# A three-stage fp32 block on one core: the identity matrix loaded earlier, head loads in two parts, no sums on GpSimd

## Chip, cores and metric

The kernel runs on one core of one Trainium2 chip. The metric is the device time of one execution in microseconds (us), the median of several.

## What is computed

Attention with a local window and a few global keys, then a token and channel mixer, then a gated block, on batch 2, 8 heads, 768 tokens, head size 64 (so 512 channels). Cut to what matters:

```python
scores = (q @ k.T) / 8 - slope[h] * dist            # kept where key < n_global or 0 <= i-j < n_local
a = softmax(scores);  x = heads_to_channels(a @ v)  # x: (2, 768, 512)
u = x + (relu(x.T @ w_tok1) @ w_tok2).T             # token mixing
y = u + relu(u @ w_ch1) @ w_ch2                     # channel mixing, 1536 wide
h = relu(y @ w_in); g, v = h[:, :512], h[:, 512:]
out = (g * (w_spatial @ layernorm(v) + b)) @ w_out
```

The weights arrive as 64-bit floats (w_spatial as 32-bit) and are split on the chip into a high and a low part, so every large product is three matmuls (`mm3`, lines 341 to 343).

## The kernel before

**Stages.** The first stage, about the first 107 us, is attention with the token mixing (`tok`) woven in. The 16 heads are 8 pairs; a pair has three units of 256 queries (`unit`), and `group` takes two units at a time, so there are 12 groups. Per unit TensorE makes scores (L479), VectorE adds the bias and finds the maximum (L496), ScalarE does exp (L500), TensorE transposes the result with the identity matrix `ident` (L506), ScalarE or VectorE copies it out as `pt` (L346). Per group, TensorE multiplies the copies with the values (L534, "main", and L544, "rest"), and the result goes back through another transpose (L567). Then come channel mixing for batch 0 and batch 1 (`ch`, to about 340 us) and the gated block (`mlp2`).

**What sets the order.** Every piece of work is an `Op` with its possible engines and their costs in us. `Plan.run` simulates the engines and writes the program in the order in which it places the pieces; each engine then executes its own row in that order, whatever arrives when. `RAW_AT` holds earliest planned starts for loads, `free` the time at which an engine is first free in the plan, `dma()` the planned time of a transfer (plus a lag of 2.1 us on SP). Eighty dummy matmuls of 256 columns (L593, "fillers") stand in the plan wherever TensorE has nothing else.

**Loads.** All are issued by SP, in order. The first head pair is loaded by hand in `build` (L240 to L247) in four pieces into `first`: two pieces of queries and keys, a third piece of keys, then the values (1088 KB); `ident` (64 KB) comes last. The other seven pairs are loaded by `load_raw` (L441), one transfer of 1936 KB each, into two buffers `raw`: a load can start when the pair two before it has been used up by L544. Weights pass through staging buffers (L386) and are split by ScalarE (L387, L388) and VectorE (L389 to L394, L352).

**Sums.** `tts` names the engines for a sum or difference of two tensors: GpSimd or VectorE. Residual sums at the end of `ch` and some splits use it (all at L352). At the end of `ch` for one batch, `ch` for the other batch goes on, and its `L786` on VectorE feeds TensorE.

Of the kernel before, what the change touches and what calls it, by code (L numbers as in the profile page):

```python
# [51 lines left out]

WARM = 9

RAW_AT = {(0, 1): 5.5, (0, 2): 12.5}
IDLE = 80, 4.0, 0.2

SWITCH, TURN = 0.16, 2.0
# [37 lines left out]
class Plan:  # L96
# [41 lines left out]
    def run(self):  # L138
        after = {}
        for q in self.slots.values():  # L140
            for b in q:
                if b.first is None:
                    continue
                for u in b.users:
                    if u is not b.first:
                        after.setdefault(u, set()).add(b.first)
                if b.opener is not None and b.opener.plan is self:
                    b.first.deps.add(b.opener)
                if b.evicts is not None:
                    b.first.deps.update(b.evicts.users)  # L150
                if b.prior is not None and b.prior.first is not b.first:
                    after.setdefault(b.first, set()).add(b.prior.first)
                b.first.deps.discard(b.first)
        for o in self.ops:
            both = {d for d in o.deps | after.get(o, set()) if d.plan is self}
            o.left = len(both)
            for d in both:
                d.kids.append((o, d in o.deps))
        order = [o for o in self.ops if o.left == 0]
        wait = {o: o.left for o in self.ops}  # L160
        for o in order:
            for k, _ in o.kids:
                wait[k] -= 1
                if wait[k] == 0:
                    order.append(k)
        for o in reversed(order):
            e, c = min(o.where, key=lambda x: x[1])
            o.rank = c + max((k.rank + (self.LAG[e] if data else 0.0) for k, data in o.kids), default=0.0)
            o.key = (PK * o.pri - o.rank, o.n)
        free = dict.fromkeys(self.LAG, 4.0)  # L170
        avail = [o for o in self.ops if o.left == 0]
        mode = "full"
        while avail:
            best, t_min, picks = None, None, []
            for o in avail:
                _, s, e, c = min((max(free[e], o.ready) + c * (1.0 + o.lam.get(e, 0.0)), max(free[e], o.ready), e, c) for e, c in o.where)
                picks.append((s, o, e, c))
            t_min = min(p[0] for p in picks)
            s, o, e, c = min((p for p in picks if p[0] <= t_min), key=lambda p: (p[1].key[0] + TURN * (p[1].mode not in (None, mode)), p[1].n))
            avail.remove(o)  # L180
            if o.mode not in (None, mode):
                c += SWITCH
            mode = o.mode or mode
            free[e] = s + c
            o.fn(e)
            for k, data in o.kids:
                if data:
                    same = len(k.where) == 1 and k.where[0][0] == e and e != "SP"
                    k.ready = max(k.ready, s + c + (0.0 if same and e == "PE" else 0.06 if same else self.LAG[e]))
                k.left -= 1  # L190
                if k.left == 0:
                    avail.append(k)
        assert all(o.left == 0 for o in self.ops)
# [10 lines left out]
def pool(n):  # L204
    return ("POOL", n * 0.0023 + 0.05)


def dma(nbytes):
    return ("SP", max(nbytes / 360e3, 0.5))


def mm(n, count):
# [3 lines left out]
def build(tc, A, out):  # L216
    nc = tc.nc
    V, SC, SY = nc.vector, nc.scalar, nc.sync
    with ExitStack() as top:
# [19 lines left out]
        with tc.manual_schedule():  # L239
            SY.dma_start(nt, A["n"].partition_broadcast(P))  # L240
            load0 = lambda c0, c1: SY.dma_start(raw0[:, c0:c1], A["qkv"][0, 0, :, c0:c1])
            SY.dma_start(rj, A["rj"])
            load0(512, 1056)
            load0(0, 512)
            load0(1056, QK)
            load0(QK, RAW)
            SY.dma_start(ident, A["ident"])  # L247
            V.memset(zero, 0.0)
            for x in shift:
                V.memset(x, 0.0)  # L250
            V.memset(epst, 1e-6)
            SC.activation(warm, epst, AF.Exp)
            with tc.tile_pool(name="dp", bufs=1, space=bass.MemoryType.PSUM) as dp:
                dummy = dp.tile([P, 512], F32, name="dummy")
                for _ in range(WARM):
                    nc.tensor.matmul(dummy, lhsT=zero, rhs=zero[:, 0:1].broadcast_to([P, 512]), start=True, stop=True)

            gl, ll = nt[:, 0:1], nt[:, 2:3]
            V.tensor_scalar(out=fl[:, 0:1], in0=gl, scalar1=0.0, scalar2=None, op0=ALU.is_ge)
            V.tensor_scalar(out=fl[:, 1:2], in0=ll, scalar1=1.0, scalar2=None, op0=ALU.is_ge)  # L260
            V.scalar_tensor_tensor(out=fl[:, 0:1], in0=gl, scalar=float(GMAX), in1=fl[:, 0:1], op0=ALU.is_le, op1=ALU.mult)
            V.scalar_tensor_tensor(out=fl[:, 1:2], in0=ll, scalar=float(LMAX), in1=fl[:, 1:2], op0=ALU.is_le, op1=ALU.mult)
            V.tensor_tensor(out=fi, in0=fl[:, 0:1], in1=fl[:, 1:2], op=ALU.mult)
            V.tensor_copy(fl[:, 2:3], gl)
            V.tensor_copy(fl[:, 3:4], ll)
            gl, ll = fl[:, 2:3], fl[:, 3:4]
            far = stgp.tile([P, 1024], BF16, tag="c", name="far")[:, :BW]
            glb = stgp.tile([P, 1024], BF16, tag="a", name="glb")[:, :BW]
            V.tensor_scalar(out=far, in0=rj[:, 0], scalar1=ll, scalar2=BIG, op0=ALU.is_ge, op1=ALU.mult)
            V.tensor_scalar(out=glb, in0=rj[:, 1], scalar1=gl, scalar2=BIG, op0=ALU.is_ge, op1=ALU.mult)  # L270
            V.tensor_tensor(out=far, in0=far, in1=rj[:, 0], op=ALU.max)
            V.scalar_tensor_tensor(out=dist, in0=glb, scalar=ll, in1=far, op0=ALU.max, op1=ALU.min)
# [10 lines left out]
class Arm:  # L283
# [68 lines left out]
        self.eng[e].tensor_tensor(out=o, in0=a, in1=b, op=op)  # L352

    def tts(self, n):
        return [pool(n), dve(n)]

    def split(self, hi, lo, src, n, rk, hk, lk):

# [72 lines left out]
    def load_raw(self, b, hp):  # L431
# [5 lines left out]
            self.rawk[b, hp] = None  # L437
            return
        r = self.raws[b, hp] = self.buf("att", "raw", [P, RAW], F32, 2)
        self.rawk[b, hp] = (r,)  # L440
        o = self.plan.op([dma(P * RAW * 4)], lambda e: self.SY.dma_start(r(), self.A["qkv"][b, hp, :, :RAW]), [], [(r,)], RAWP if (b, hp) != (0, 1) else None)  # L441
        o.ready = RAW_AT.get((b, hp), 0.0)

    def band_bias(self, b, h):
        bias = self.bias[b, h] = self.buf("att", f"bias{h % 2}", [P, BW], F32, 2)
# [17 lines left out]
    def scores(self, units):  # L463
# [4 lines left out]
        for k, (b, hp, u) in enumerate(units):  # L468
            tiles = self.tiles(u)

            def make(e, k=k, b=b, hp=hp, tiles=tiles):
                raw = self.raws[b, hp]
                for t, o, w in tiles:
                    for x in range(2):
                        k0 = S + (160 * t - P + D * x if t else 0)
                        q0 = q_at(t) + D * x
                        for i in range(2):
# [1 line left out]
                            T.matmul(banks[k][i]()[x * D:x * D + D, o:o + w], lhsT=r[:, q0:q0 + D], rhs=r[:, k0:k0 + w],  # L479
                                     start=True, stop=True)  # L480

            self.plan.op([("PE", sum(w for _, _, w in tiles) * 0.00175)], make, [self.rawk[b, hp] or ("raw0", "ab"[u > 0])],
                         [(x,) for x in banks[k]], mode="quarters")
        return banks

# [27 lines left out]
    def group(self, units):  # L513
# [31 lines left out]
                                     rhs=pts[k][h]()[r, 2 * P + x * D:2 * P + x * D + D], start=False,  # L545
                                     stop=(x == 1 and k == max(z for z in range(2) if units[z][2] or j)))

        rk = [self.rawk[b, hp] or ("raw0", "v") for b, hp, _ in units]
        ps = [(p,) for x in pts for p in x]
        op([("PE", 0.88)], main, ps + rk, [(c,) for c in cs], mode="columns")  # L550
        op([("PE", 0.44)], rest, ps + rk, [(c,) for c in cs], mode="quarters")
# [490 lines left out]
```

## Time and profile before

| | us |
|---|---|
| median of 3 runs | 484.67 (484.59 to 484.98) |
| the profiled execution | 484.22, of it span 482.3 |
| TensorE busy | 470.4 |
| VectorE busy | 292.3 |
| ScalarE busy | 208.5 |
| GpSimd busy | 29.7 |

The span runs from the first to the last instruction. Matmuls are pipelined, so TensorE counts as busy while it moves through waits shorter than a matmul's length; a wait that shows as idle is a true one. Fillers count as busy too. A wait in brackets behind a row is the idle time of that engine just before it, and who ended it.

### The profile page before, as it was taken

Reading aid. Unit: us, or ns where it says so; the run is one execution under the profiler, and the core shown is the slowest. Engines: PE = TensorE matmul, PEld = TensorE weight load, DVE = VectorE, ACT = ScalarE, POOL = GpSimd, SP = SyncE. Lnnn points to the kernel's source line nnn. Section 1 sums busy time; section 2 is a strip of 40 time slices with the busy share of each in tenths; the row PEclk is TensorE's granted clock in tenths of the full one; section 3 lists DMA queues with packets and bytes.
Section 4 is the critical chain, followed back from the end, with each engine's and each line's share of the span. In section 5 each row is a group of like instructions: output and inputs, shape, how many; then the busy total and the mean of one; then the engine's idle time right before and its main releaser. Section 6 shows DMA issues by size and latency. Waiting matters only on the chain.

```text
span 482.3 us, 8996 instructions
## 1 busy us (share of the span) xinstructions
PE 470.4 (98%) x3557; PEld 413.0 (86%) x3557; DVE 292.3 (61%) x773; ACT 208.5 (43%) x527; POOL 29.7 (6%) x29
## 2 busy tenths in 40 slices
PE   7999999999999999999999999999999999999996
PEld 4788888789988888888888888888999988899985
DVE  4899998779988986012986854236961512722520
ACT  3999898897645544110333501113521122411121
POOL 0110001000000000000500000003330000000000
PEclk9999999999999999999999999999999999999999
DMA  7944927413343442000033311110000011000012
GB/s 275 376 171 167 371 91 278 187 63 119 116 148 114 146 152 97 0 1 1 0 102 128 121 65 37 63 34 0 2 0 1 1 67 65 1 0 2 0 45 93
DMA packets 10993, 44.66 MB, mean 93 GB/s; under 512 B 1344, under 2 KB 1856, under 8 KB 9920
## 3 DMA queue, kind: packets, MB, share of 16 engines
q1 hardware_dynamic: 10944, 44.01, 25.5%
q8 instruction: 30, 0.49, 0.4%
q14 instruction: 19, 0.16, 0.1%
HBM read 40.86 MB, written 3.15 MB: 91 GB/s over the span
## 4 chain that ended last, share of the span: by engine, by line
PE 82%; DVE 7%; DMA 6%; ACT 1%; issue 1%; POOL 1%; SPq 0%; ACTq 0%; DVEq 0%; POOLq 0%
PE p L341 23%; PE p L343 23%; PE p L342 23%; PE p L506 3%; PE p L479 3%; PE p L534 2%; DMA raw<-in_qkv 2%; DMA raw<-in_w_in 2%; DVE first L352 2%; PE p L544 1%; DMA raw<-in_wt 1%; PE p L593 1%; PE p L567 1%; DVE uy0l L352 1%; PE p L738 1%
## 5 line engine op out<-in xcount | busy, mean ns | idle before, releaser
L341 PE MATMUL p<-raw,w 128*128 128x512 f32 (+1 forms) x192 | 64.8, 338 | 0.0
L342 PE MATMUL p<-raw,w 128*128 128x512 f32 (+1 forms) x192 | 64.7, 337 | 0.0
L785 ACT ACTIVATE raw<-p 128x512 fp32r<-128x512 f32 (+1 forms) x48 | 23.6, 491 | 95.0 <-PE p L343 88.1
L343 PE MATMUL p<-raw,w 128*128 128x512 f32 (+1 forms) x192 | 64.6, 337 | 0.0
L786 DVE SCALAR_TENSOR_TENSOR raw<-p,raw 128x512 fp32r<-128x512 f32 (+1 forms) x48 | 26.0, 552 | 37.4 <-ACT raw L785 37.1
L341 PE MATMUL p<-uy1h,w 128*128 128x512 f32 (+2 forms) x128 | 43.3, 338 | 1.6 <-DVE raw L786 1.6
L343 PE MATMUL p<-uy1h,w 128*128 128x512 f32 (+2 forms) x128 | 43.2, 337 | 0.0
L343 PE MATMUL p<-uy0h,w 128*128 128x512 f32 (+2 forms) x128 | 43.1, 337 | 0.0
L342 PE MATMUL p<-uy1l,w 128*128 128x512 f32 (+2 forms) x128 | 43.1, 337 | 0.0
L342 PE MATMUL p<-uy0l,w 128*128 128x512 f32 (+2 forms) x128 | 43.1, 337 | 0.0
L341 PE MATMUL p<-uy0h,w 128*128 128x512 f32 (+2 forms) x128 | 43.1, 336 | 0.0
L500 ACT ACTIVATE e<-e,nm 128x192 f32<-128x192 f32 (+1 forms) x96 | 41.9, 445 | 1.3 <-DVE nm L496 1.3
L387 ACT ACTIVATE c<-raw 128x512 bf16<-128x512 bf16 x42 | 28.3, 673 | 30.1 <-DMA raw<-in_w_in 17.4
L343 PEld LDWEIGHTS p<-raw,w 128*128 128x128 f32 x192 | 36.1, 188 | 4.2
L341 PEld LDWEIGHTS p<-raw,w 128*128 128x128 f32 x192 | 36.1, 188 | 4.1
L342 PEld LDWEIGHTS p<-raw,w 128*128 128x128 f32 x192 | 36.1, 188 | 4.0
L352 DVE TENSOR_TENSOR c<-p,bsp 128x384 f32<-128x384 f32 x16 | 8.9, 558 | 39.7 <-PE p L343 39.7
L496 DVE CUSTOM_DVE_ANT_0 e<-p,bias 128x192 f32<-128x192 f32 (+1 forms) x96 | 27.4, 341 | 5.1 <-PE p L479 5.1
L394 DVE SCALAR_TENSOR_TENSOR a<-raw,q 128x512 f32<-128x512 uint32 x42 | 29.0, 691 | 0.5
L352 DVE TENSOR_TENSOR a<-a,c 128x512 f32<-128x512 f32 x42 | 28.8, 686 | 0.4
L388 ACT ACTIVATE c<-raw 128x512 bf16<-128x512 bf16 x42 | 28.1, 670 | 0.0
L341 PEld LDWEIGHTS p<-uy1h,w 128*128 128x128 f32 x128 | 24.1, 188 | 4.5 <-DVE raw L786 2.4
(163 smaller groups left out, 1086.5 us busy)
## 6 DMA issues: line engine op xcount, KB each, us to landing
raw<-in_qkv SPq DMA_DIRECT2D x7, 1936.0 KB, 9.8
raw<-in_wch SPq DMA_DIRECT2D x24, 512.0 KB, 3.7
raw<-in_w_in SPq DMA_DIRECT2D x8, 512.0 KB, 4.1
raw<-in_wt SPq DMA_DIRECT2D x6, 512.0 KB, 5.4
out<-a SPq DMA_DIRECT2D x11, 256.0 KB, 2.0
raw<-in_w_sp SPq DMA_DIRECT2D x6, 384.0 KB, 2.9
raw<-in_w_out SPq DMA_DIRECT2D x4, 512.0 KB, 3.9
first<-in_qkv SPq DMA_DIRECT2D x1, 1088.0 KB, 7.2
```

The costliest lines, as they stand in the source:

```text
L341: T.matmul(o, lhsT=w[0], rhs=x[0], start=first, stop=False)
L342: T.matmul(o, lhsT=w[0], rhs=x[1], start=False, stop=False)
L343: T.matmul(o, lhsT=w[1], rhs=x[0], start=False, stop=last)
L352: self.eng[e].tensor_tensor(out=o, in0=a, in1=b, op=op)
L387: op([act(n)], lambda e: self.SC.mul(pw(), top(), 2.0 ** -112), [(w,)], [(c, 0)])
L388: op([act(n)], lambda e: self.SC.activation(sg(), top(), AF.Sign), [(w,)], [(c, 1)])
L394: op([dve(n)], lambda e: V.scalar_tensor_tensor(out=aa(), in0=mid(), scalar=2.0 ** -36, in1=qq(), op0=ALU.mult, op1=ALU.mult), [(w,), (q,) ...
L479: T.matmul(banks[k][i]()[x * D:x * D + D, o:o + w], lhsT=r[:, q0:q0 + D], rhs=r[:, k0:k0 + w], start=True, stop=True)
L496: op([dve(w)], lambda e, j=j, o=o, w=w, bs=bs: V.tensor_tensor_reduce(out=e_()[:, o:o + w], in0=s()[:, o:o + w], in1=bias()[:, bs], scale= ...
L500: op([act(w, 0.2)], lambda e, j=j, o=o, w=w: SC.activation(e_()[:, o:o + w], e_()[:, o:o + w], AF.Exp, bias=nm()[:, j:j + 1], scale=-1.0, ...
L785: op([act(n)], lambda e, m=m, r=r, sl=sl, n=n: SC.activation(r()[:, 0, sl], m()[:, :n], AF.Relu), [(m,)], [(r, z, 0)])
L786: op([dve(n)], lambda e, m=m, r=r, sl=sl, n=n: V.scalar_tensor_tensor(out=r()[:, 1, sl], in0=m()[:, :n], scalar=0.0, in1=f32(r()[:, 0, sl] ...
```

## The change

Five edits. `ident` is loaded ahead of the third piece of keys and of the values. `load_raw` issues two transfers per pair, 848 KB of queries and keys and 1088 KB of values, each with its own dependency, so that scores wait for the first alone and L534 for the second. The plan's numbers change: the earliest planned start of the first part of pair 1 (8.5; none for the rest, `RAW_AT`), SP free from 7.5 instead of 4.0 (`START`), and a planned rate of 400 instead of 360 KB per us. `tts` leaves only VectorE. Lines move down by up to five: L500 of before is L505 of after, L387 is L390, L346 is L349, L441 is L445.

```diff
-RAW_AT = {(0, 1): 5.5, (0, 2): 12.5}
+RAW_AT = {(1, 0): 8.5}
+START = 7.5
...
         free = dict.fromkeys(self.LAG, 4.0)
+        free["SP"] = START
...
-    return ("SP", max(nbytes / 360e3, 0.5))
+    return ("SP", max(nbytes / 400e3, 0.5))
...
             load0(0, 512)
+            SY.dma_start(ident, A["ident"])
             load0(1056, QK)
             load0(QK, RAW)
-            SY.dma_start(ident, A["ident"])
...
     def tts(self, n):
-        return [pool(n), dve(n)]
+        return [dve(n)]
...
-        self.rawk[b, hp] = (r,)
-        o = self.plan.op([dma(P * RAW * 4)], lambda e: self.SY.dma_start(r(), self.A["qkv"][b, hp, :, :RAW]), [], [(r,)], RAWP if (b, hp) != (0, 1) else None)
-        o.ready = RAW_AT.get((b, hp), 0.0)
+        self.rawk[b, hp] = r
+        for k, sl in enumerate((slice(0, QK), slice(QK, RAW))):
+            o = self.plan.op([dma(P * (sl.stop - sl.start) * 4)], lambda e, sl=sl: self.SY.dma_start(r()[:, sl], self.A["qkv"][b, hp, :, sl]),
+                             [], [(r, k)])
+            o.ready = RAW_AT.get((hp, k), 0.0) if b == 0 else 0.0
```

The scores then read key `(rawk, 0)`, the products with the values `(rawk, 1)`. Since the plan is written anew, the order moves in the whole first stage. Of the fillers, 34 instead of 40 now stand ahead of the first L534, and of the transposes (L506) 12 instead of 15.

ScalarE's row at the start of before, from the first exps on: the exps of unit 0, then the first split of a weight piece (L387, L388, which read the first `in_wt` transfer), then the exps of unit 1.

```order
L500 ACTIVATE e,rs<-e,nm 128x128 x2
L500 ACTIVATE e,rs<-e,nm 128x192 x2
L387 ACTIVATE c<-raw 128x512
L388 ACTIVATE c<-raw 128x512
L500 ACTIVATE e,rs<-e,nm 128x192 x2
L346 COPY pt<-p_221 128x384
L500 ACTIVATE e,rs<-e,nm 128x192 x2
```

The same place of after:

```order
L505 ACTIVATE e,rs<-e,nm 128x128 x2
L505 ACTIVATE e,rs<-e,nm 128x192 x4
L349 COPY pt<-p_215 128x384
L505 ACTIVATE e,rs<-e,nm 128x192 x2
L390 ACTIVATE c<-raw 128x512
L349 COPY pt<-p_258 128x384
L349 COPY pt<-p_272 128x384
```

The four exps of unit 1 and one copy stand ahead of the weight's split now.

SP's row of before, from the third piece of the first pair on:

```order
L241 DMA first<-in_qkv 128x640
L241 DMA first<-in_qkv 128x2176
L247 DMA ident<-in_ident 128x128
L276 TENSOR_LOAD fi
L276 ISA x2
L277 COMPARE_AND_BRANCH
L386 DMA raw<-in_wt 128x2048 x2
L441 DMA raw<-in_qkv 128x3872
L386 DMA raw<-in_wt 128x2048
L441 DMA raw<-in_qkv 128x3872
```

And of after:

```order
L248 DMA ident<-in_ident 128x128
L244 DMA first<-in_qkv 128x640
L244 DMA first<-in_qkv 128x2176
L279 TENSOR_LOAD fi
L279 ISA x2
L280 COMPARE_AND_BRANCH
L389 DMA raw<-in_wt 128x2048
L445 DMA raw<-in_qkv 128x1696
L445 DMA raw<-in_qkv 128x2176
L445 DMA raw<-in_qkv 128x1696
L445 DMA raw<-in_qkv 128x2176
L389 DMA raw<-in_wt 128x2048 x2
```

The four halves of pairs 1 and 2 now stand ahead of the second weight piece; the first of them directly behind the first weight piece.

VectorE's row of before at the end of `ch` for batch 0 (`first` is the sum there, `uy0h` and `uy0l` its two parts, `raw` the next block's input to TensorE):

```order
L352 TENSOR_TENSOR first<-first,uy0l 128x768 x2
L352 TENSOR_TENSOR uy0l<-first,uy0h 128x768
L346 CAST uy0h<-first 128x768
L352 TENSOR_TENSOR uy0l<-first,uy0h 128x768 x2
L346 CAST w_3276<-a 128x512 x2
L352 TENSOR_TENSOR w_3276<-a,w_3276 128x512
L786 SCALAR_TENSOR_TENSOR raw<-p_3223,raw 128x512
```

And of after:

```order
L355 TENSOR_TENSOR first<-first,uy0l 128x768 x4
L355 TENSOR_TENSOR uy0l<-first,uy0h 128x768 x3
L349 CAST w_3288<-a 128x512
L791 SCALAR_TENSOR_TENSOR raw<-p_3228,raw 128x512
```

Two more sums stand on VectorE ahead of L786 (three came from GpSimd, one difference went behind it); a cast of 768, one of 512 and a split of `w` left this place.

## Rows read from the trace of the kernel before

**Rows 1.** Busy time of the engines, share of the span, instructions (page, part 1).
```profile
PE 470.4 (98%) x3557; PEld 413.0 (86%) x3557; DVE 292.3 (61%) x773; ACT 208.5 (43%) x527; POOL 29.7 (6%) x29
```

**Rows 2.** What TensorE waited for: us in total, times, longest us.
```profile
PE p L506 <- DMA ident<-in_ident: 1.7, 1, 1.7
PE p L341 <- DVE raw L786: 1.6, 2, 1.2
PE p L506 <- ACT pt L346: 1.0, 1, 1.0
PE p L479 <- DMA raw<-in_qkv: 1.0, 1, 1.0
...
PE p L534 <- DVE first L574: 0.5, 1, 0.5
PE p L343 <- POOL vn L352: 0.4, 1, 0.4
```

**Rows 3.** Timeline of the opening: start us, us, engine, what, [idle before].
```profile
6.37 0.61 SPq L441 DMA_DIRECT2D raw<-in_qkv  x1
...
8.14 0.44 ACT L500 ACTIVATE e<-e,nm 128x192 f32<-128x192 f32 x1
...
8.91 0.36 DVE L496 CUSTOM_DVE_ANT_0 e<-p,bias 128x192 f32<-128x192 f32 x1 [1.26 <-PE p L479]
...
11.72 0.66 ACT L387 ACTIVATE c<-raw 128x512 bf16<-128x512 bf16 x1 [3.04 <-DMA raw<-in_wt]
...
13.73 0.45 ACT L346 COPY pt<-p 128x384 f32<-128x384 f32 x1
...
17.18 1.14 PE L534 MATMUL p<-pt,first 128*64 128x128 f32 x28
```

**Rows 4.** Transfers issued in the first 10 us: count, KB, us to landing.
```profile
raw<-in_qkv SPq DMA_DIRECT2D x1, 1936.0 KB, 12.2
first<-in_qkv SPq DMA_DIRECT2D x1, 1088.0 KB, 7.2
raw<-in_wt SPq DMA_DIRECT2D x2, 512.0 KB, 6.8
...
ident<-in_ident SPq DMA_DIRECT2D x1, 64.0 KB, 6.9
```

**Rows 5.** Later transfers: weight pieces, the seven loads of L441, one in the chain.
```profile
raw<-in_wch SPq DMA_DIRECT2D x24, 512.0 KB, 3.7
...
DMA to landing us min/median/max: 7.3/9.8/12.2
...
74.11 10.59 DMA raw<-in_qkv
```

**Rows 6.** Fillers: in the chain (start, us), and per stretch (busy, count).
```profile
16.03 0.89 PE p L593 x8
...
20.00:41.00 21.00, 6.24 (x40) 3.81 (x39) 1.00 0.62 224
```

**Rows 7.** Attention, 15 to 107 us: busy PE, PEld, DVE, ACT, POOL, clock, DMA.
```profile
15.00:107.00 92.00, 90.15 (x1420) 76.40 (x1418) 81.80 (x327) 86.37 (x289) 7.08 (x12) 1.00 0.55 204
```

**Rows 8.** Timeline at the end of `ch` for batch 0, and one undisturbed sum.
```profile
230.02 4.39 POOL L352 TENSOR_TENSOR first<-first,uy0l 128x768 f32<-128x768 f32 x2 [154.93 <-issue]
...
231.72 3.50 DVE L352 TENSOR_TENSOR first<-first,uy0l 128x768 f32<-128x768 f32 x2
235.15 2.61 DVE L352 TENSOR_TENSOR uy0l<-first,uy0h 128x768 fp32r<-128x768 f32 x1
...
241.16 1.01 DVE L786 SCALAR_TENSOR_TENSOR raw<-p,raw 128x512 fp32r<-128x512 f32 x2
...
241.89 0.50 PE L341 MATMUL p<-uy1h,w 128*128 128x512 f32 x1 [1.24 <-DVE raw L786]
...
349.10 0.93 DVE L352 TENSOR_TENSOR first<-first,uy1l 128x768 f32<-128x768 f32 x1
```

**Rows 9.** The last sum on GpSimd ahead of the gated product.
```profile
353.05 1.93 POOL L352 TENSOR_TENSOR vn<-a,vn 128x512 fp32r<-128x512 f32 x1 [1.30 <-DVE vn L346]
```

More of the change, by code (lines that the diff above doesn't have):

```diff
@@ L480, in make @@
                                      start=True, stop=True)
-            self.plan.op([("PE", sum(w for _, _, w in tiles) * 0.00175)], make, [self.rawk[b, hp] or ("raw0", "ab"[u > 0])],
+            self.plan.op([("PE", sum(w for _, _, w in tiles) * 0.00175)], make, [(self.rawk[b, hp], 0) if self.rawk[b, hp] else ("raw0", "ab"[u > 0])],
                          [(x,) for x in banks[k]], mode="quarters")
@@ L546, in rest @@
                                      stop=(x == 1 and k == max(z for z in range(2) if units[z][2] or j)))
-        rk = [self.rawk[b, hp] or ("raw0", "v") for b, hp, _ in units]
+        rk = [(self.rawk[b, hp], 1) if self.rawk[b, hp] else ("raw0", "v") for b, hp, _ in units]
         ps = [(p,) for x in pts for p in x]
```

## Prediction, made before the result was known

> **What bounds the kernel now.** I read the busy shares first. TensorE is busy for 470.4 of the 482.3 us of the span [rows 1], so a change can shorten the run only by taking TensorE's idle time away, or its useless work. Next I read what TensorE waited for [rows 2]. Six waits matter: 1.7 us for the identity matrix, 1.0 for a copy `pt`, both in the opening; 1.0 for the load of a head pair; 0.5 for VectorE in attention; 1.6 in two pieces for VectorE's L786, behind the end of `ch`; 0.4 for a sum on GpSimd. That is 6.2 us, and it is the ceiling on what this change can bring as long as the 80 fillers stay. About 0.11 us each (0.89 for eight [rows 6]), they come to 8.8 us, half of them (40) between 20 and 41 us [rows 6]: there TensorE is ahead of ScalarE and VectorE, and has no real work to put into the gap. Last I looked at who else is full in attention: from 15 to 107 us, a stretch of 92.0, ScalarE is busy for 86.4 and VectorE for 81.8 [rows 7]. ScalarE has 5.6 us of room there, no more. That is where a gain can be lost again.
>
> **The opening.** The identity matrix is 64 KB, but it landed 6.9 us after its issue because it stood behind 1088 KB of values, which took 7.2 [rows 4]. TensorE's first transpose waited 1.7 us for it. The second wait, 1.0 us for `pt`, has another cause. ScalarE's last exp of unit 0 ends at about 8.6, and then its row holds L387, the split of a weight that landed only at 11.7: ScalarE idles 3.04 us, and the exps of unit 1, for which VectorE was ready long before, stand behind it [rows 3]. The new order of ScalarE puts those exps and a copy ahead of L387. I walk it: VectorE hands over unit 1 from about 9.3; four exps at 0.44 and one copy at 0.45 end at 11.5; L387 finds its weight at 11.7 and takes 0.66; two copies at 0.45 end at 13.3 [rows 3]. The first L534 can start at about 13.35 instead of 17.18, which is 3.83 earlier. Of this, 0.66 is six fillers that now stand behind it, and so do three transposes. The rest, 3.2 less the transposes, agrees with the two waits, 1.7 and 1.0 [rows 2]. I take **-2.7**. What is late next: the queries and keys of pair 1, which the scores behind the first L534 want at 13.35 + 1.1 = 14.45. In before, the first weight landed at 11.7, and the second with the whole pair, 2448 KB together, by 6.4 + 12.2 = 18.6 [rows 3, 4]: 2.8 us per 1000 KB. In after, the 848 KB stand directly behind the first weight, so they land at 11.7 + 2.4 = 14.1, just in time. Moving `ident` ahead delays the third piece of keys by 64 KB, 0.2 us at this rate; 14 fillers stand in front of its scores, 1.5 us of work that needs no load, so I cost that at nothing; without that cover it is 0.2.
>
> **Loads in two parts.** The load of pair 6 was issued at 74.1 and landed 10.6 us later [rows 5], and TensorE lost 1.0 us there [rows 2]. With two parts the scores need only the first. From 512 KB in 3.7 us and the shortest whole load, 1936 KB in 7.3 [rows 5], a part of 848 KB takes 3.7 + 336 x 3.6 / 1424 = 4.55 us when little stands ahead of it. So that wait goes: -1.0. But the new order also uses the room: it places the first scores of pairs 3, 4 and 6 only one group behind the release of their buffer, on a planned 848 KB (868,352 bytes) / 400 + 2.1 = 4.27 us. By the rows each is 0.3 late, and more with weights in the queue ahead. The bounds are nothing, where TensorE is late itself, and 7.3 - 4.27 = 3.0 each, if a half lands no sooner than the quickest whole load. I take 0.4 each, close to the interpolated row: +1.2. Together **+0.2**. The values, 1088 KB, land about when the whole load did and are needed one group later than the scores.
>
> The Trainium skill, "DMA: Bandwidth & Descriptors", section "Anatomy of one DMA — SWDGE (gpsimd) path", gives a transfer about 2.0 us fixed plus its bytes over 436 GB/s, measured on another issuing path than SP's. An estimate by it is 4.0 us for the first part, less than planned, so the +1.2 would be nothing and the whole sum -5.35 (479.3 us); its estimate for 512 KB is 3.2 where the trace has 3.7, so I stay with the rows.
>
> **Rest of attention.** Of its 92.0 us there TensorE idles 1.85 [rows 7]; without the load's 1.0, some 0.8 is left (0.5 of it for L574 [rows 2]), which hangs on the old order. I take **-0.5**, between 0 and -0.8. Against it stands ScalarE. By its own work it is not 3.8 us ahead at the first L534: three exps, a copy and L388, 2.4 us, have moved behind that point, so its lead is 1.4. TensorE's lead is 2.7. Where ScalarE decides, between 13 and 41 us and again at the end, up to 1.3 us of the opening is given back; against that, fillers may be displaced and weights' splits can move to a later stage. Bounds 0 and 1.3; I take **+0.5**, nearer the lower one, since 46 fillers still stand behind the first L534 as a cushion.
>
> **No sums on GpSimd.** GpSimd did 12 of these, and I look at the two places where TensorE waited. At the end of `ch` for batch 0, GpSimd ran two sums of 768 columns in 4.39 us, and beside them VectorE's own two took 3.50 and the next 2.61, where an undisturbed one takes 0.93 with overlap [rows 8], a pitch of about 0.87. So the engines held each other up. In after, VectorE does four sums and three differences ahead of L786: 7 x 0.87 = 6.1 us from 231.7, then a cast, about 0.4: L786 can start at about 238.2 instead of 241.16. TensorE was ready for it at 241.89 - 1.24 = 240.65 [rows 8]; even 1.5 us later L786 would be in time. The wait goes: **-1.24**. The second piece of that wait, 0.4 [rows 2], I leave as it is. At 353 the last sum on GpSimd took 1.93 [rows 9] and TensorE waited 0.4; on VectorE it is 0.87 x 512 / 768 = 0.6: **-0.4**. The cover for the added VectorE work elsewhere is that TensorE works through matmuls of the other batch; if it is gone, three added sums cost 2.6 us.
>
> **Sum.** -2.7 + 0.2 - 0.5 + 0.5 - 1.24 - 0.4 = -4.15 us (rounded). The profiled execution took 484.22 (span 482.3 and 1.9 around it), so 480.07; the median of the runs lies 0.45 above that execution: **480.5 us**. In what follows 0.2% (about 1 us) is what a measurement of this kernel can tell from no change.
>
> **Rivals.**
> - *ScalarE keeps the opening's gain.* If attention runs at ScalarE's pace, the term of 0.5 becomes 1.3 and the 0.5 from the other waits is not had, and the tight loads cost 2.0 instead of 1.2: 480.5 + 0.8 + 0.5 + 0.8 = 482.6. For it: 86.4 of 92.0 [rows 7]. Against it: TensorE idles only 1.85 of those 92 us beside it, and has fillers to spare.
> - *The first parts land late* (the slower side). If a half load needs 7.3 us, as the quickest whole one did, the three tight pairs cost 3.0 each instead of 0.4: 480.5 + 3 x 2.6 = 488.3. It turns the sign from 1.8 us per tight pair on (4.15 / 3 + 0.4). For it: the loads took up to 12.2 in the opening [rows 4]. Against it: there 1024 KB of weights stood ahead, and since 512 KB take 3.7 and 1936 KB 7.3 [rows 5], half the bytes should cost clearly less.
> - *VectorE becomes late.* If its sums do not get cheaper without GpSimd, L786 comes 2.6 later instead of 3 earlier, and TensorE waits 1.24 + 2.6: 480.5 + 1.24 + 2.6 = 484.3, no change. Against it: sums of the same size at 0.93 without GpSimd beside them.
> - *`ident` does not come in time.* If it lands with the values as before, the 1.7 stays: 482.2. Against it: it stands behind 690 KB instead of 2098.
>
> **How the numbers follow.** Forecast 0.56, ScalarE 0.22, late parts 0.07, VectorE 0.07, `ident` 0.04; 0.04 is left for a gain near the ceiling (478.4). The forecast's own bounds are 479.0 to 482.0 (terms at their better and worse ends). To hold 8 in 10, the range takes in the second case and most of the ceiling: 478.6 to 483.2. Faster by over 0.2%: 0.56 + 0.22 + 0.04 + 0.04 = 0.86; same 0.07; slower 0.07.
>
> **What would show it.** In the profile after: no wait of TensorE for `ident`; ScalarE without the 3 us gap ahead of its first weight split, and the first L534 at 13 to 14 us; waits of TensorE for `in_qkv` below 0.6 us each at three or four places; end of attention (last L534) 2.5 to 4 us earlier; seven sums in a row on VectorE at 0.87 and no wait for L786 behind them. It is wrong if the waits for `in_qkv` add up to over 4 us, if TensorE's idle time in attention grows by as much as the opening lost, or if the waits for L786 grow.

## The result, and the profile after

The changed kernel takes 477.11 us (476.65 to 477.99, four runs) against 484.63: a ratio of 0.9845, 95% interval 0.9829 to 0.986, so 7.5 us less. Measured again among the experiments it took 477.92 against 484.13 (ratio 0.9876, 0.9857 to 0.9896). The prediction had 480.5 with a range from 478.6 to 483.2. The direction was right; the gain is larger than forecast, and larger than the 6.2 us that I had called the ceiling.

The page after, busy time of the engines (answers to [rows 1]); the span is 474.9 instead of 482.3:

```profile
PE 469.1 (99%) x3557; PEld 414.3 (87%) x3557; DVE 291.0 (61%) x781; ACT 210.3 (44%) x531; POOL 7.8 (2%) x17
```

What TensorE waited for, after (answers to [rows 2]):

```profile
PE dummy L259 <- DVE epst L254: 1.0, 1, 1.0
PE p L484 <- DMA raw<-in_qkv: 0.6, 1, 0.6
```

All of the six waits are gone but 0.6 of the load's. TensorE's idle time in the span fell from 482.3 - 470.4 = 11.9 to 474.9 - 469.1 = 5.8, by 6.1 us. The span fell by 7.4. So 1.3 us came out of time that counted as busy, although all 3557 matmuls are still there.

The opening after, from the timeline (answers to [rows 3]; start us, us, engine, what, idle before):

```profile
8.97 0.87 PE L511 MATMUL p<-ident,e 128*128 128x128 f32 x6
...
12.45 0.67 ACT L390 ACTIVATE c<-raw 128x512 bf16<-128x512 bf16 x1 [0.73 <-DMA raw<-in_wt]
13.03 0.84 ACT L349 COPY pt<-p 128x384 f32<-128x384 f32 x2
...
13.27 1.32 PE L539 MATMUL p<-pt,first 128*64 128x128 f32 x28
14.64 0.89 PE L484 MATMUL p<-raw 64*64 64x128 f32 x16
```

ScalarE's gap ahead of its first weight split is 0.73 instead of 3.04, and the first of the products with the values starts at 13.27 instead of 17.18, near the 13.35 of the walk.

Attention, from the first to the last of these products, in the windows view: before and after (stretch, its length, then busy PE, PEld, DVE, ACT, POOL, clock, DMA):

```profile
17.20:104.30 87.10, 85.25 (x1331) 72.14 (x1330) 76.97 (x312) 81.94 (x277) 5.69 (x10) 1.00 0.55 204
```

```profile
13.30:98.80 85.50, 84.77 (x1330) 73.02 (x1329) 79.98 (x324) 81.91 (x283) 6.39 (x11) 1.00 0.61 227
```

ScalarE does the same 81.9 us of work in 1.6 us less. The lead of 3.9 us at the first product did not shrink on the way; at the last one it is 5.5.

The end of `ch` for batch 0 on VectorE after (answers to [rows 8]):

```profile
227.13 3.56 DVE L355 TENSOR_TENSOR first<-first,uy0l 128x768 f32<-128x768 f32 x4
230.61 2.69 DVE L355 TENSOR_TENSOR uy0l<-first,uy0h 128x768 fp32r<-128x768 f32 x3
233.34 0.43 DVE L349 CAST w<-a 128x512 fp32r<-128x512 f32 x1
234.03 0.69 DVE L791 SCALAR_TENSOR_TENSOR raw<-p,raw 128x512 fp32r<-128x512 f32 x1 [0.27 <-ACT raw L790]
```

Seven sums and differences in 6.2 us, 0.89 each beside an estimate of 0.87, and the bias step behind them even waits 0.27 for ScalarE. TensorE waits for nothing there.

### The profile page after: what moved, and what is told of

Its sections match the earlier page's. It is cut to its first block, busy times and chain, and to the rows that moved or that the text cites. A ratio compares the mean times of both kernels' runs of the same rounds, so it can differ in the third digit from the quotient of the medians.

```text
span 474.9 us, 8988 instructions
## 1 busy us (share of the span) xinstructions
PE 469.1 (99%) x3557; PEld 414.3 (87%) x3557; DVE 291.0 (61%) x781; ACT 210.3 (44%) x531; POOL 7.8 (2%) x17
## 3 DMA queue, kind: packets, MB, share of 16 engines
HBM read 40.86 MB, written 3.15 MB: 93 GB/s over the span
## 4 chain that ended last, share of the span: by engine, by line
PE 98%; DMA 1%; DVE 0%; issue 0%
PE p L344 27%; PE p L345 27%; PE p L346 27%; PE p L484 4%; PE p L511 4%; PE p L539 3%; PE p L598 2%; PE p L549 1%; DMA raw<-in_qkv 1%; PE p L743 1%; PE p L572 1%; PE dummy L259 1%; DVE c L349 0%; DVE zero L251 0%; DVE shift L253 0%
## 5 line engine op out<-in xcount | busy, mean ns | idle before, releaser
L346 PE MATMUL p<-raw,w 128*128 128x512 f32 (+1 forms) x192 | 64.6, 336 | 0.0
L505 ACT ACTIVATE e<-e,nm 128x192 f32<-128x192 f32 (+1 forms) x96 | 42.4, 455 | 4.3 <-DVE nm L501 4.3
L346 PE MATMUL p<-uy1h,w 128*128 128x512 f32 (+2 forms) x128 | 43.2, 337 | 0.0
L346 PE MATMUL p<-uy0h,w 128*128 128x512 f32 (+2 forms) x128 | 43.2, 337 | 0.0
L390 ACT ACTIVATE c<-raw 128x512 bf16<-128x512 bf16 x42 | 28.6, 680 | 28.3 <-DMA raw<-in_w_in 12.6
L346 PEld LDWEIGHTS p<-raw,w 128*128 128x128 f32 x192 | 36.1, 188 | 4.2
L355 DVE TENSOR_TENSOR w<-a,w 128x512 fp32r<-128x512 f32 x36 | 24.6, 685 | 2.8 <-ACT w L349 2.7
```

The lines of the kernel that those rows point to most:

```text
L346: T.matmul(o, lhsT=w[1], rhs=x[0], start=False, stop=last)
L390: op([act(n)], lambda e: self.SC.mul(pw(), top(), 2.0 ** -112), [(w,)], [(c, 0)])
L505: op([act(w, 0.2)], lambda e, j=j, o=o, w=w: SC.activation(e_()[:, o:o + w], e_()[:, o:o + w], AF.Exp, bias=nm()[:, j:j + 1], scale=-1.0, ...
```

## The experiments

My theory after the result (A): the opening's whole shift is kept, because what stood in its way was ScalarE's order and because fillers cost nothing; and a wait of TensorE costs more than the idle time that its row shows. Rivals: each edit has a price of its own, as the prediction's terms had it; ScalarE sets the pace; the gain is one lucky order. In the table, time is the median of the runs, first and last are the starts of the first and the last timeline row of products with the values (L534 before, L539 after; a row is some 30 matmuls) in the profiled run, and rest is the span less last. All times in us.

| kernel | time | before beside it | first | last | rest |
|---|---|---|---|---|---|
| before | 484.67 | | 17.18 | 104.28 | 378.0 |
| after | 477.11 | 484.63 | 13.27 | 98.80 | 376.1 |
| e9 after again | 477.92 | 484.13 | 13.31 | 98.78 | 376.1 |
| e1 before, ident early | 485.78 | 484.33 | 20.20 | 107.74 | 378.0 |
| e2 before, sums on VectorE | 482.32 | 484.33 | 17.46 | 105.59 | 375.4 |
| e3 after, sums on GpSimd too | 480.07 | 484.33 | 13.16 | 99.70 | 378.6 |
| e4 after, ident late | 478.54 | 484.33 | 17.04 | 101.95 | 376.0 |
| e5 after, single loads | 487.23 | 484.18 | 13.22 | 111.33 | 374.9 |
| e6 after, old numbers | 485.04 | 484.18 | 19.98 | 106.24 | 377.2 |
| e7 after, more on ScalarE | 480.01 | 484.18 | 13.00 | 101.63 | 376.1 |
| e8 after, 40 fillers planned | 480.84 | 484.18 | 13.76 | 100.88 | 378.0 |
| e10 after, less on ScalarE | 476.87 | 484.13 | 13.23 | 98.82 | 376.2 |
| e11 before, more on ScalarE | 487.19 | 484.13 | 18.01 | 107.97 | 377.2 |
| e12 after, start 8.0 | 479.99 | 484.13 | 13.52 | 102.59 | 375.2 |
| e13 after, no late fillers | 478.36 | 484.59 | 13.60 | 99.65 | 376.0 |
| e14 before, no late fillers | 483.50 | 484.59 | 17.45 | 103.81 | 377.8 |
| e15 after, rate 420 | 478.59 | 484.59 | 13.22 | 102.44 | 374.7 |
| e16 after, start 7.0 | 481.01 | 484.59 | 14.19 | 103.63 | 375.6 |

### The sums, alone and taken back

```diff
 def tts(self, n):
-    return [pool(n), dve(n)]
+    return [dve(n)]
```

> The kernel before with one edit: sums and differences only on VectorE, none on GpSimd. Attention keeps its order. Theory A (a wait of TensorE costs more than the idle time that its row shows, since matmuls are pipelined: from start to start the three waits concerned, 1.24 and 0.3 for L786 and 0.38 for vn, take 1.52, 0.59 and 0.65 us more than undisturbed ones): all three go, -2.76 us, to 481.9 (481.5 to 482.2). Rival 1 (the terms of the prediction, by idle time: -1.24 and -0.4, the second wait for L786 stays): -1.64, to 483.0. Rival 2 (VectorE becomes late behind its added sums): the waits for L786 grow, 484.3 or more.

> The kernel after with one edit taken back: sums may go to GpSimd again; attention keeps the new order. Theory A (waits cost 0.25 us each above their idle time): the same waits come back, TensorE's busy time grows by about 0.8 beside an idle time of about 2, and the time rises from 477.1 by 2.5 to 2.9, to 479.6 to 480.0. Rival (cost is idle time only): +1.6 to 2.0, 478.7 to 479.1. If the sums had nothing to do with the gain: 477.1.

Alone the edit gives a ratio of 0.9947 (0.9929 to 0.9964), which is 2.6 us; by the medians it is 2.0, between theory and rival. Taken back from after it costs 2.2 to 3.0 (480.07 beside the two measurements of after). The traces are sharper, since attention's order is the same in each pair: the rest is 2.6 shorter (378.0 to 375.4) in the one and 2.5 longer (376.1 to 378.6) in the other. Counted from start to start on TensorE, both differences are 2.4; the remaining 0.1 or 0.2 lies behind its last matmul. The idle time concerned was 2.0 [rows 2]. Where the other 0.4 sits is seen in before, on TensorE, at the first of these waits:

```profile
240.03 0.39 PE L342 MATMUL p<-raw,w 128*128 128x512 f32 x1
240.25 0.40 PE L343 MATMUL p<-raw,w 128*128 128x512 f32 x1
241.89 0.50 PE L341 MATMUL p<-uy1h,w 128*128 128x512 f32 x1 [1.24 <-DVE raw L786]
242.23 0.39 PE L342 MATMUL p<-uy1l,w 128*128 128x512 f32 x1
242.46 0.39 PE L343 MATMUL p<-uy1h,w 128*128 128x512 f32 x1
```

A matmul of 512 columns lasts 0.39 but the next one starts 0.23 later. From 240.25 to 241.89 are 1.64, so 1.41 more than undisturbed; the next start is again 0.11 late. The wait cost 1.52 and shows as 1.24: the overlap of two matmuls is lost, and a row counts it as busy. In e2, where the wait is gone, the matmuls at this place of TensorE's row come 1.51 closer together. That part of theory A stands, with less than the 2.76 it expected; rival 1 (1.64, by the terms of the prediction) is too small in both traces.

### The identity matrix, alone and taken back

```diff
             load0(0, 512)
+            SY.dma_start(ident, A["ident"])
             load0(1056, QK)
             load0(QK, RAW)
-            SY.dma_start(ident, A["ident"])
```

> The kernel before with one edit: the identity matrix is loaded ahead of the third piece of keys and of the values; no other instruction moves on any engine. Theory A (what gains in the opening is ScalarE's new order; the identity matrix alone only moves the wait): TensorE's wait of 1.7 us for ident goes, but the transposes behind it then wait for the copy pt, which stands on ScalarE behind the weight's split at 11.72 us; that wait grows from 1.0 to about 2.7, the first L534 stays at 17.2 us (within 0.2), and the time stays at 484.6 (484.2 to 484.9). Rival (each wait is a cost of its own): the first L534 comes 1.7 earlier, at 15.5, and the time is 482.8.

> The kernel after with one edit taken back: the identity matrix is loaded last again, behind the values; no other instruction moves. Theory A (in the new order ScalarE is no longer held up by the weight, so here the identity matrix does set the opening): TensorE waits 1.6 to 1.8 us for ident ahead of its first transpose (at about 10.6 instead of 8.97), the first L539 comes at 14.6 to 15.0 instead of 13.27, and the time is 478.4 to 478.9. Rival (the new order has the slack to hide it, and the early load is worth nothing even there): within 0.4 of 477.1.

Alone it gains nothing; it loses (ratio 1.0035, 1.0018 to 1.0052). TensorE's waits in e1:

```profile
PE p L506 <- ACT pt L346: 3.8, 1, 3.8
```

The wait for `ident` is gone and the one for `pt` has grown from 1.0 to 3.8, since ScalarE stands in front of its weight split, which in this run came later still (13.26):

```profile
13.26 0.65 ACT L387 ACTIVATE c<-raw 128x512 bf16<-128x512 bf16 x1 [4.13 <-DMA raw<-in_wt]
```

So the mechanism is as expected, and the loss beside it was not. The loss goes with TensorE's granted clock: the four executions of e1 with a mean clock of 0.998 or more took 484.00 to 485.44, like before, and the eight at 0.996 or less 485.12 to 487.75; the profiled one is among the eight. In after, with the new order, the same load does matter: put last again, it brings back a wait of 1.9 for `ident` and 0.8 for a piece of keys. The time is 0.6 to 1.4 above after's two medians (ratio 0.9882, 0.9862 to 0.9902); 478.54 lies where theory A had it, but the intervals are too wide to hold the rival off by the time alone. In the profiled run the first product slid by 3.77, not by 1.3 to 1.7, for a reason told in the last section. Of these 3.77 the last product still has 3.15 and the span 3.1: what the opening loses is passed on nearly whole. The clock divides e4's executions too: three at 1.000 took 478.10 to 478.54, two at 0.996, the profiled one among them, 479.90 and 480.19. So the late `ident` by itself costs 0.4 to 1.3 us (478.36 beside after's two medians), and 1.7 more come where the clock falls.

### Loads in two parts, and the plan's numbers

e5 takes the two parts back and keeps the numbers:

```diff
-        self.rawk[b, hp] = r
-        for k, sl in enumerate((slice(0, QK), slice(QK, RAW))):
...
+        self.rawk[b, hp] = (r,)
+        o = self.plan.op([dma(P * RAW * 4)], lambda e: self.SY.dma_start(r(), self.A["qkv"][b, hp, :, :RAW]), [], [(r,)], ...)
```

e6 takes the numbers back and keeps all else:

```diff
-RAW_AT = {(1, 0): 8.5}
-START = 7.5
+RAW_AT = {(1, 0): 5.5, (2, 0): 12.5}
+START = 4.0
...
-    return ("SP", max(nbytes / 400e3, 0.5))
+    return ("SP", max(nbytes / 360e3, 0.5))
```

> The kernel after with one part taken back: each head pair is again one transfer of 1936 KB (the planned numbers of after stay, so the order is planned anew; ScalarE's row in the opening keeps the exps of unit 1 ahead of the weight's split). Theory A (the first part alone is what the scores need in time): the first L539 stays at 13.3 (within 0.4), but TensorE waits for in_qkv at pair 1, since 1936 KB behind the first weight land at about 17.5 instead of 14.1, and again at one or two later pairs (planned 6.9 us to landing, the loads of before took 7.3 to 12.2): 2 to 5 us of such waits, time 479.0 to 481.5. Rival (the order of ScalarE alone carries the gain): waits for in_qkv below 1 us in all and 477.0 to 477.8.

> The kernel after with only the plan's numbers of before (SP free from 4.0, 360 KB per us, earliest starts 5.5 and 12.5); identity early, loads in two parts and sums on VectorE stay. Its row of ScalarE has the weight's split ahead of the exps of unit 1 again. Theory A (the planned start of SP is what moved ScalarE's row, and that row makes the opening): ScalarE idles 3 to 4 us ahead of L390, TensorE waits 2.7 to 3.8 us for pt, the first L539 comes at 16.5 to 17.5, time 479.5 to 481.0 (the opening's 3 us lost, the rest kept). Rival (the early identity and the two parts carry it): 477.1 within 0.6.

Both cost far more than I expected: 1.0063 (1.004 to 1.0087) and 1.0017 (0.9994 to 1.004) against before, so each of them alone undoes the whole gain and, with the sums' 2.5 still in it, more. e6 shows why the numbers are there: the weight split is back in front of unit 1's exps.

```profile
11.75 0.28 PE L598 MATMUL p<-zero 128*128 128x256 bf16 x1
...
12.84 0.65 ACT L390 ACTIVATE c<-raw 128x512 bf16<-128x512 bf16 x1 [3.59 <-DMA raw<-in_wt]
...
13.95 0.44 ACT L505 ACTIVATE e<-e,nm 128x192 f32<-128x192 f32 x1
...
15.33 0.55 PE L511 MATMUL p<-ident,e 128*128 128x128 f32 x3 [3.30 <-ACT pt L349]
...
19.98 1.24 PE L539 MATMUL p<-pt,first 128*64 128x128 f32 x28
```

The first product stands at 19.98, later than in before; this is later than the 16.5 to 17.5 expected, and it is passed on again. A lower clock from 16 to 20 us has a part in it (last section). In e5 the opening stays (13.22), and then attention takes 98.1 us instead of 85.5, with waits of TensorE for many things:

```profile
PE p L482 <- DMA raw<-in_qkv: 1.9, 2, 1.3
PE p L482 <- DVE rs L563: 1.3, 1, 1.3
PE p L344 <- DVE raw L789: 1.0, 1, 1.0
PE p L509 <- ACT pt L349: 1.0, 2, 0.5
```

These add up to less than the 12.6 lost. TensorE's granted clock fell twice in it, between 56 and 68 us, but that is not the bulk: two executions at a mean clock of 1.000 took 485.91 and 486.94. The order was planned anew, so e5 does not say what the two parts are worth in one given order; that stays open.

### Is ScalarE the bound?

More work on ScalarE (e7 on after, e11 on before), and less (e10, which leaves out the exp of 64 columns at 65 places, so that its output is not the block's):

```diff
                 SC.activation(e_()[:, o:o + w], ..., accum_out=rs()[:, k, j, h % 2])
+                if j == 0 and h % 2 == 0 and (b, h) != (0, 0):
+                    SC.mul(self.spare, self.dist[:, :P], 1.0)
```

> The kernel after with 21 more copies of 128 x 128 on ScalarE, one behind the first exp of every second head in each unit of attention but those of the first pair; they read dist, write a spare tile that nothing reads, and nothing else moves. About 0.2 us each, 4.2 us in all. Theory A (ScalarE is nearly full but TensorE sets the pace, with some lead of ScalarE to eat up): below +1.5 us, 477.1 to 478.6. Rival (ScalarE sets the pace of attention, as my second case had it): each added us shows, +3.5 to +4.5, 480.6 to 481.6.

> The kernel before with the same 21 copies on ScalarE as in the run with more ScalarE work on after (3.4 us more of busy time, which cost 2.9 there). Theory A (before, ScalarE idled 5.2 us between the first and the last L534, after only 3.6: the change uses up its room): 0.5 to 1.8 us. Rival 1 (ScalarE set the pace before as well): 2.6 to 3.2. Rival 2 (there was room for all of it): below 0.3.

```diff
+                v = o + 64 if w == KW and h + b > 1 else o
-                SC.activation(e_()[:, o:o + w], e_()[:, o:o + w], AF.Exp, ...)
+                SC.activation(e_()[:, v:o + w], e_()[:, v:o + w], AF.Exp, ...)
```

> The kernel after with 65 exps of attention on 128 instead of 192 columns (the first 64 columns of a block keep their raw scores, so the probabilities differ); nothing moves. About 0.05 us each less on ScalarE, 3.3 us in all. Theory A (TensorE is the bound of after, and ScalarE only just keeps up): below 0.6 us of gain. Rival (ScalarE sets the pace of attention, and each us on it shows in both directions): -2 to -3.

Added work shows: in after, attention gets 3.1 longer (88.63 instead of 85.53), and the time 2.1 to 2.9, which lies between theory and rival. ScalarE is busy there for 86.31 instead of 81.91; of these 4.4 us the copies account for 3.4 (210.3 to 213.7 in the whole span), the rest is mostly other work that now falls into the longer stretch. In before, 3.0 more (84.95 where it was 81.94) make it 2.9 longer, and the time 3.1; there theory A falls, and with it my reading of [rows 7]: the 5.2 us that ScalarE idled in before were no room at all. Work taken away does not show in the trace: e10 has 2.1 less (79.76) and the same stretch (85.59 beside 85.53) and rest; its median is 1.0 below e9's, within the intervals (0.9848, 0.9827 to 0.9869). So in after, as I read it, both engines are at their limit in the order that is planned: ScalarE has hardly a lead to give away, and TensorE hardly idle time to fill. Windows of e7 and e10:

```profile
13.00:101.63 88.63, 86.33 (x1329) 72.87 (x1329) 80.53 (x323) 86.31 (x305) 5.37 (x11) 1.00 0.59 221
```

```profile
13.23:98.82 85.59, 84.67 (x1330) 73.43 (x1329) 79.70 (x324) 79.76 (x284) 6.36 (x11) 1.00 0.61 225
```

### What a filler costs

e13 and e14 leave out the fillers behind the first product, with everything else in its place (the cut is e13's; e14 has 40 for 34); e8 plans with 40 from the start:

```diff
-            o = plan.op([mm(256, 1)], lambda e: self.T.matmul(
+            o = plan.op([mm(256, 1)], lambda e, i=i: i < 34 and self.T.matmul(
```

> The kernel after without the 46 fillers that stand behind the first L539; every other instruction keeps its place on every engine. They take 46 x 0.11 = 5.1 us. Theory A (a filler stands where TensorE would wait, so it is free, and moving six of them behind the first L534 cost nothing): TensorE's idle time grows by 3.5 to 5, the last L539 stays within 0.6 of 98.8, time 477.0 to 478.7. Rival 1 (fillers hold work up, as the prediction's deduction of 0.66 for six had it): -2 to -5, 473 to 476. Rival 2 (the granted clock falls where the fillers had stood): one stretch at 0.5 costs 1.7, 478.7 or more.

> The kernel before without the 40 fillers that stand behind the first L534, 4.4 us; every other instruction keeps its place. Theory A (free): within 0.6 of before beside it, idle time up by 3 to 4.4. Rival 1 (they hold work up): -2 to -4. Rival 2 (clock): +1.7 or more.

```diff
-IDLE = 80, 4.0, 0.2
+IDLE = 40, 4.0, 0.2
```

> The kernel after with 40 fillers instead of 80; the order is planned anew. Theory A (fillers stand where TensorE would wait, so they cost next to nothing; taking 40 away turns 4.4 us of them into idle time): TensorE's idle time in the first 60 us grows by 2 to 4.4 us, time within 0.7 of 477.1. Rival 1 (they displace work): -1.5 to -4.4, 472.7 to 475.6. Rival 2 (idle time in the opening lets TensorE's granted clock fall to half for a stretch, as in the run with the identity matrix late, where it was 0.50 from 12 to 14 us): +1 to +3, 478.1 to 480.1.

Leaving out 46 fillers from after changes the time by +0.4 to +1.2 (ratio 0.9872, 0.9826 to 0.9918), and TensorE's idle time grows from 5.8 to 475.7 - 466.3 = 9.4: they were no cost. They may have been worth something: two of e13's four executions took 477.07 and 477.48 at a mean clock of 0.999 and 0.998, the other two 479.25 and 479.52 at 0.996. That fits rival 2 (the clock falls without them) in those two, but the one trace is of the first pair, so where it fell is not shown. In before, leaving out 40 gains 1.1 us (ratio 0.9979, 0.9963 to 0.9995), a quarter of their 4.4: more than theory A's 0.6 and less than rival 1's 2 to 4, so there some of them did hold work up. Where the fillers stood, TensorE now waits for what they had hidden, as the waits of e13 show:

```profile
PE p L484 <- DMA raw<-in_qkv: 1.7, 1, 1.7
PE p L511 <- ACT pt L349: 1.4, 3, 0.6
...
PE p L511 <- ACT e L505: 1.0, 2, 0.6
```

So a filler that moves behind the first product is, in after, no work that is put off. e8 went against theory A, at +2.9 to +3.7, but without the clock of rival 2 (1.00 all through attention): planning with 40 fillers gave another order, with waits of 1.7 for `in_qkv` and 1.2 for `ct`. As a test of fillers it is void; as a test of orders it belongs to the next group.

### How far the gain is this one order

e9 is after unchanged; e12 and e16 move the planned start, e15 the planned rate:

```diff
-RAW_AT = {(1, 0): 8.5}
-START = 7.5
+RAW_AT = {(1, 0): 9.0}
+START = 8.0
```

```diff
-START = 7.5
+START = 7.0
```

```diff
-    return ("SP", max(nbytes / 400e3, 0.5))
+    return ("SP", max(nbytes / 420e3, 0.5))
```

> The kernel after, unchanged, as the mark for the runs beside it. Ratio to before 0.983 to 0.986, as it was; no wait of TensorE but those for the start and 0.4 to 0.9 for in_qkv. If the granted clock makes the difference between chips, its times spread over more than 2 us, as those of the runs with the identity matrix late or with the old numbers did.

> The kernel after with SP planned free from 8.0 instead of 7.5 (first part of pair 1 from 9.0 instead of 8.5). The order is planned anew: ScalarE's first weight split stands behind three more exps, so its idle time of 0.73 us ahead of L390 should go. Theory A (that row of ScalarE is what the number is for): first L539 at 13.0 to 13.5, no ScalarE idle time at L390, 476.0 to 477.5. Rival (any new order of attention costs or gains some us elsewhere, as with 40 fillers): 478 to 481.

> The kernel after with a planned rate of 420 instead of 400 KB per us. SP's row and the opening stay; the order differs from the middle of attention on. Theory A (the gain outside the opening hangs on one planned order, and a neighbour may lose or win some us): off from 477.5 by 1 to 3 us either way, with other waits at other places. Rival (the edits themselves carry it, and neighbours are alike): within 0.8 of 477.5.

> The kernel after with SP planned free from 7.0 instead of 7.5. Two weight pieces instead of one stand ahead of pair 1's first part, so it lands 512 KB later, at about 15.9 instead of 14.5 us, while its scores are wanted at 14.6. Theory A (in after this part arrives just in time, as the walk had it): a wait for in_qkv of 1.0 to 1.6 there, and +1 to +3 in all with the changed order, 478.5 to 480.5. Rival (there is slack): no such wait, 477 to 478.5.

e9 came out at a ratio of 0.9876, a little outside the expected 0.983 to 0.986, and its wait for `in_qkv` was 1.1 where at most 0.9 was expected. The neighbours 8.0 and 7.0 are slower than after: 479.99 (ratio 0.9916, 0.9898 to 0.9934) and 481.01 (0.9924, 0.9896 to 0.9951); 420e3 is at 478.59 (0.9869, 0.9832 to 0.9906), above both medians of after but not apart from it. Their openings stay within 1 us of 13.3, the rest is even shorter, and what they lose lies in the middle, where first to last takes 89.1 (e12), 89.4 (e16) and 89.2 (e15) instead of 85.5. A part of that is work moved ahead: 9, 6 and 18 fewer matmuls stand behind the last product, and the rest is 0.9, 0.5 and 1.4 shorter. e12 has the opening that theory A asked for, with no idle time of ScalarE at L390, and is slower all the same: there the rival was right. e16 has the wait that the walk gave it, but smaller, since its own scores came later:

```profile
16.50 0.89 PE L484 MATMUL p<-raw 64*64 64x128 f32 x16 [0.55 <-DMA raw<-in_qkv]
```

So 1 to 4 us of the gain hang on the one order that these numbers give, and no reading of edits in the diff could have priced them. No variant that does the whole work beats after.

## Why the prediction was off, step by step

**The ceiling.** I added up the idle time of six waits, 6.2, and called it what the change can bring at most. Idle time did fall by 6.1. But a wait costs its idle time and the overlap of two matmuls besides. In the rest of the kernel that is shown (2.4 between TensorE's starts for 2.0 of idle time); that the remaining 0.9 of the 1.3 us has the same cause in the opening and in attention is likely, but only argued.

**The opening, -2.7 forecast, -3.9 measured.** The first half of the walk was right: ScalarE's exps and copy end where I had them. The second half came out right partly by luck: the weight landed at 12.4, not at 11.7, so the two copies behind its split ended at 13.87 instead of 13.3, and the first product stands at 13.27 because it began while they still ran. Pair 1's first part landed at 14.51 for an estimate of 14.1, its scores started at 14.64. The step that failed is the deduction of 0.66 for six fillers and some tenths for three transposes. Of the 3.9, TensorE's idle time is 2.9 and its busy time 1.0, about what the moved fillers and transposes take; I had deducted these as work still to do. But fillers fill waits; without them there is a wait (e13, e14), and attention, which took them in and gave nine other matmuls off, was busy for 84.77 instead of 85.25. And I compared 3.2 with the two visible waits, 2.7, and took the smaller number, which is the error of the ceiling once more.

**Loads in two parts, +0.2 forecast, about -0.4 measured.** The durations were right: a first part with nothing ahead of it took 4.4 and 4.5 us at two places, for an interpolated 4.55; with a weight piece under way it took 5.0, 6.3 and 6.5. The Trainium skill, "DMA: Bandwidth & Descriptors", section "Anatomy of one DMA — SWDGE (gpsimd) path", gave an estimate of 4.0: the trace is longer even with nothing ahead, by 0.4 to 0.5. The failed step is to charge 0.4 at each of three places. At pairs 3 and 6 the part landed 0.6 and 1.1 ahead of its scores, since TensorE came to them later than planned; only pair 4, behind a weight piece, made it wait:

```profile
45.82 1.05 PE L539 MATMUL p<-pt,raw 128*64 128x64 f32 x30
47.49 0.78 PE L484 MATMUL p<-raw 64*64 64x128 f32 x16 [0.62 <-DMA raw<-in_qkv]
```

**Rest of attention, -0.5, and ScalarE, +0.5.** The small waits went as said. ScalarE gave nothing back. I had taken its idle time for its lead. The runs on both kernels show that work added to it makes attention longer by 0.9 to 1.0 us per us (3.1 for 3.4, 2.9 for 3.0), so the rival's mechanism is real; but the gain of the opening was ScalarE's gain too (its gap of 3.04 went to 0.73), which is, as I read it, why there was nothing to give back. First to last product is 1.6 shorter; 9 matmuls more stand behind the last one, and the rest is 0.7 longer than in e2, which has after's sums and before's attention. Net this stretch gained 0.9 where I had 0.2 lost with the loads in it.

**Sums, -1.64 forecast, -2.5 to -2.6 measured.** The failed step is to count the idle time of two waits. The walk on VectorE was right to 0.1 us. Two things were missing: the second wait for L786, which I left as it was, went too; and each wait was worth more than its idle time.

**The sum.** -3.9 - 0.9 - 2.6 = -7.4, the fall of the span. Against my terms: opening 1.2 too small, attention 1.1, sums 1.0. All three errors point one way, and two of them are the same one: I capped terms by visible idle time. None of the rivals came about: of late parts the waits show 0.6 us, of a late VectorE or a late `ident` nothing.

**The range** had its low end at 478.6 because it was built from that ceiling. The chance of 0.04 for a gain near it was too small for the same reason.

## What to carry to other kernels

Price a wait by the starts of the matmuls around it, less their undisturbed spacing, and not by the idle time in the row; and don't call the sum of idle times a ceiling. Before counting moved filler work as a cost, ask what stands there without it. An idle engine with a fixed order has no room unless its idle time lies where the added work would go; and a planner's number changes the whole order, so measure its neighbours before crediting the idea behind it.

## What the hardware showed unexpectedly

A long wait of TensorE in the opening can have a second price. In e1 it idled 3.84 us up to 15.76, and the granted clock fell from its upper level to half, that is from 2.4 to 1.2 GHz, for part of the next 4 us (windows of TensorE: stretch, length, busy, clock, DMA):

```profile
14.00:16.00 2.00, 0.24 (x2) 1.00 0.99 411
16.00:18.00 2.00, 2.00 (x14) 0.65 0.61 186
18.00:20.00 2.00, 2.00 (x12) 0.50 1.10 394
20.00:22.00 2.00, 2.00 (x65) 1.00 0.99 403
```

In those 4 us (0.35 + 0.5) x 2 = 1.7 us of matmul time were lost. e4 had waits of 0.84 and 1.87 between 8 and 11.4, and the same fall:

```profile
10.00:12.00 2.00, 0.59 (x3) 0.70 1.03 424
12.00:14.00 2.00, 2.00 (x12) 0.50 1.03 434
```

Seven fillers took 1.67 there and 0.94 in after; e6, e11 and e14 show the same behind waits of 3.3, 1.9 and 2.1. This is why e4's first product came 3.77 later for 2.7 us of waits, and e1 lost where I expected no change; in e1 the runs spread from 484.0 to 487.75, and none of e6's ten has a mean clock above 0.996. Waits of 1.7 and 1.0 in the profile of before left the clock at 1.00, as did 1.15 and 0.55 in e16's opening. With the opening full, after's clock fell only behind its last matmul (which ended at 471.0; 0.50 from 474 on).

The price is not always paid. In e14, before's opening, the clock fell as well:

```profile
12.00:14.00 2.00, 2.00 (x18) 0.50 1.03 439
```

Yet its first product stands at 17.45 beside 17.18: the wait of 1.0 for `pt`, which TensorE would have had next, is gone there, so the slower work ran in time that would have been idle. It is the same for before itself: of its 59 executions beside the experiments, 29 have a mean clock of 0.996 or less and a median of 484.5, the other 30 one of 484.2. So of the 7.5 us of this change the clock can have given a few tenths at most.
